# Gate/up of the last layer: the fourth product split into seven half-size ones, LayerNorm steps in three parts, w_down block sums behind the last row writes

## The chip, the cores and the metric

The kernel runs on one core of one Trainium2 chip. The metric is the device time of one execution in microseconds (us). The kernel before takes 1454.52 us, the median of three runs (1454.23 to 1454.56).

## What is computed

Two blocks alternate, A, B, A, B, over a residual stream x of 2048 tokens by 1024 channels (bf16). Every block sees the layer-normalised x and adds its result to x:

```
x = x + A(layernorm(x), wqkv, wo)      # linear attention, 32 heads
x = x + B(layernorm(x), w_gate, w_up, w_down)
x = x + A(layernorm(x), wqkv, wo)
x = x + B(layernorm(x), w_gate, w_up, w_down)

B: g = x @ w_gate; u = x @ w_up        # 1024 x 3584 each
   return (g * u) @ w_down             # 3584 x 1024
```

The same weights serve both B blocks. "First layer" and "last layer" below mean the first and second B block (with the A block ahead of each).

## The kernel before, in words

All work is recorded operation by operation in one list (class `_Prog`), each with the bytes and PSUM banks it reads and writes; waits are worked out from these. The order on every engine is the order of recording, so it is written out by hand, and every engine works strictly through its own list. All DMAs go through SyncE's list.

**The products of block B** use a Winograd form of Strassen's scheme: a 2x2 block product as seven block products. For a *pass* (`ps_` 0 or 1) of 1024 tokens, `gateup` handles 14 *pairs*; a pair is two column tiles of w_gate (even pairs) or of w_up (odd pairs). A pair has the products 1 to 7, each over half the inner dimension and 512 tokens: four matmuls of 128x512 for each of the two column tiles A and B (`pe`, L1070, matmuls at L1071). Partial sums live in PSUM: X (banks 0, 1), Y (2, 3), Z (4, 7). ScalarE copies them to SBUF scaled (`cp`, L1074 to L1076: P1, P6, P7 each write a buffer that `fin` adds later). `fin` (F1 to F4, L1078 to L1095, on VectorE at L691) writes a gate tile of h in even pairs, and in odd pairs multiplies the up tile into it, the product on GpSimd (L1095).

**Split products.** Some of the seven products are themselves done as seven half-size products (`l2_of`, L1152 on): each over a quarter of the inner dimension and 256 tokens, two matmuls of 128x256 (`mm`, L1174). Which ones is told by `L2SETS` (L200): in the last layer products 2, 5 and 4 of both passes, in the first layer none in pass 0 and 5, 4, 2 in pass 1. A split product has the steps 1, 5, 6, 7 and the two direct parts D..A (two half products) and D..B (one):

- step 1: half product into one of the shared banks 5 or 6 (`B_L2`), then ScalarE copies it as a seed to the target bank (L1178);
- step 5: half product into the other shared bank, then ScalarE copies it to SBUF (L1190);
- step 6: half product on top of that of step 1, then VectorE adds the SBUF copy to it into the target's second half (L1181);
- step 7: half product on top of that again, then a second seed copy (L1178) and a second addition (L1181);
- the direct half products go onto the seeded target banks.

The left operands of 3, 5, 6, 7 are block sums of the weights (`sums24` for products 2 and 4, `sums5` for product 5). The first layer makes them on VectorE and stores them in DRAM; the last layer loads them (`load_s24`, `load_s5`). The right operands 4, 5, 6 are token sums (`tp_ops`).

**The order around the change** is in the strings of `ORDERS` (L201 to L206), one for each set of split products. They are run once for each pair. `P6A` is product 6 of tile A with its copy, `21` step 1 of product 2, `D2A` its direct part for tile A, `F1A` the end of output 1, `S24` and `S5` the block sums, `R` two issues of weight loads, `T0` and `T1` the ticks for background work, `H` the hook (last pair alone); a quote mark means the token belongs to the pair before, a plus to the next one.

**Background work.** `ticks0` and `ticks1` (L1637, L1666) run LayerNorm steps: a step is two statistics of 512 channels (L447), an aggregate (L451), two tiny operations on GpSimd, and for an earlier row the normalising (L469, or L466 on ScalarE) and a transpose. They run a whole step in the ticks with `u % 4 < 2`, that is in both ticks of every even pair. In the first layer's pass 0 the ticks also make block sums of w_down (`wd_tick`), and the pair's own tokens make the seven-product sums of the weights of the next pair (`prep_s`).

**The down stage** (`down`) follows each pass: h times w_down, again seven products, four of them split (`DL2`, `l2prod`, matmuls at L1553), with the half products in the order `DOPS` = 1 5 6 2 7 3 4. Its operands are sums of blocks of h (`l2sums`), made on VectorE. The hook `pre` (L1461) makes the first four of them for product 1 at `H` in the last pair. The late tokens of the last pair (`tail`) are recorded behind the down stage's first half product.

Of the kernel before, what the change touches and what calls it, by code (L numbers as in the profile page):

```python
# [180 lines left out]
def build_kernel(nc, A_x, A_wqkv, A_wo, B_w_gate, B_w_up, B_w_down, out):  # L181
# [18 lines left out]
    L2SETS = {(False, 0): "", (False, 1): "542", (True, 0): "254", (True, 1): "254"}  # L200
    ORDERS = {  # L201
# [7 lines left out]
    DOPS = "1562734"  # L209
# [3 lines left out]
    PRE = "12"  # L213
# [69 lines left out]
    P = _Prog(V_SP + NJ * 64)  # L283
# [21 lines left out]
    KL5 = [dkey("l5%d" % i) for i in range(2)]  # L305
    KTA = [dkey("ta%d" % i) for i in range(2)]
# [11 lines left out]
    p5scr = nc.dram_tensor("p5_scratch", (NJ, 128, 1024), F16, kind="Internal").ap()  # L318
    nscr = nc.dram_tensor("xn_scratch", (S, D), F16, kind="Internal").ap()

    from contextlib import ExitStack
    with ExitStack() as es:
# [120 lines left out]
        def ln_a(i, mid=None):  # L443
            j = ln_cnt[0] % 8
            ln_cnt[0] += 1
            for h in range(2):
                P.add("dve", (lambda h: lambda e: e.bn_stats(st[j][:, 6 * h:6 * h + 6], x_res[:, i, (D // 2) * h:(D // 2) * (h + 1)]))(h),  # L447
                      rd=r_x(i, (D // 2) * h, (D // 2) * (h + 1)), wr=R(O_ST[j] + 24 * h, 24))
                if mid and h == 0:
                    mid()  # L450
            P.add("dve", lambda e: e.bn_aggr(mv[j][:, 0:2], st[j]), rd=R(O_ST[j], 48), wr=R(O_MV[j], 8))  # L451
# [21 lines left out]
        class LN:  # L473

            def __init__(self, to, order):
                self.to = to
                self.order = order
                self.q_b = []
                self.q_n = []
                self.q_t = []  # L480
                self.n = 0
                self.t_next = 0
                self.use_dma = False
                self.on_act = False
                self.depth = 2

# [8 lines left out]
            def start(self, i, mid=None):  # L495
                assert i == self.n
                j = ln_a(self.order[i], mid)
# [81 lines left out]
            def flush_step(self):  # L579
# [7 lines left out]
                if self.n < NST and self.pending_ab() < 3:  # L587
                    self.start(self.n)
# [133 lines left out]

        def tp_ops(pair, prods):
            s0 = pair * 1024
            res = []
            for q in prods:
                if q == "4":
                    x, base, st_ = T4, O_T + 8192, 1024
                elif q == "5":
                    x, base, st_ = T1, O_T, 1024  # L730
                else:
                    s1 = s0 + (512 if q == "3" else 0)
                    x, base, st_ = xblk(1, s1), O_XT + 4 * S * 2 + s1 * 2, S * 2
                o = O_TP[q]
                tp = [vh(o + i * 1024, 512).rearrange("p (k s) -> p k s", s=256) for i in range(3)]
                rt = [R(o + i * 1024, 1024) for i in range(3)]
# [25 lines left out]
        def load_s24(ps_, p):  # L762
            o = O_X + (8 * ps_ + 4) * D * 2 + p % 2 * 4096
            dma(vh(o, 2048), p4scr[p], R(o, 4096), KP4[p % 2], rd=R(V_SP + p * 64, 32))
# [7 lines left out]
        def load_s5(first, ps_, p):  # L772
            v, r = sp5buf(first, ps_, p % 2)
            dma(v, p5scr[p].rearrange("p (i x) -> p i x", i=4), [x for y in r for x in y], KL5[p % 2 if ps_ and not first else 0], rd=R(V_SP + p * 64 + 32, 32))
# [20 lines left out]
        def layer_A(lnp, nxt, first):  # L795
# [198 lines left out]
            for i in range(NST):  # L994
# [17 lines left out]
                if i in (11, 12, 13, 14):  # L1012
                    stash(i - 7)
                if i == 14 and not first:
# [5 lines left out]
                while RG["tn"] < 4 and nxt.t_next > 4 + RG["tn"]:  # L1020
                    RG["tq"] += t_ops(0, RG["tn"])
                    RG["tn"] += 1
                    if RG["tn"] == 4:
                        RG["tq"] += tp_ops(0, L2SETS[not first, 0])
# [7 lines left out]
        def layer_B(lnp, nxt, first):  # L1032
# [11 lines left out]
            def pair(ps_, p, l2):  # L1044
# [68 lines left out]
                ORDER = [q for q in "2543" if q in l2]  # L1113
                DST = {"5": Y, "2": Z, "4": Z if "4" in l2 else X, "3": Y}
# [657 lines left out]
```

## Time and profile before

| | |
|---|---|
| median of three runs | 1454.52 us (1454.23 to 1454.56) |
| the profiled execution | 1453.48 us, span from first to last instruction 1451.8 us |
| first layer: gate/up pass 0 | from 240.7 us, 170.7 us |
| first layer: gate/up pass 1 | from 494.5 us, 162.9 us |
| last layer: gate/up pass 0 | from 966.8 us, 159.7 us |
| last layer: gate/up pass 1 | from 1208.2 us, 158.8 us |
| TensorE matmuls | 8250: 2128 full-size ones of gate/up (L1071), 1764 half-size ones (L1174) |

How to read it: PE is TensorE, PEld its weight loads, DVE is VectorE, ACT ScalarE, POOL GpSimd, SP (or SPq) SyncE. A row of a timeline gives the start in us from the span's start, the length in us, engine, line of the kernel, operation, what is written and read, shape, how many alike follow each other, and in brackets the idle time of the engine ahead of it with what ended it. Matmuls overlap: the length of a row runs to the modelled end of its last matmul, so the pace of TensorE is read from the distance between starts.

### The profile page before, as it was taken

To read this page: it belongs to the slowest core of one execution; us is meant where nothing else is said; L and a number is where in the kernel's file an instruction comes from. 1 tells how busy PE (TensorE), PEld (TensorE's weight loads), DVE (VectorE), ACT (ScalarE), POOL (GpSimd) and SP (SyncE) were. 2 spreads that over 40 slices of the span, in tenths; PEclk is the share of its full clock that TensorE was granted. 3 is DMA by queue.
4 is the path that set the end of the run, shared out by engine and by line. 5 is a ranking of instruction groups with operands and counts; after the bars stand their busy time and mean duration, and the time that the engine had idled before them with its cause. 6 is when DMAs were issued, how large, how long until landed. Compare 5 with 4: busy or idle time off the path is not lost.

```text
span 1451.8 us, 22020 instructions
## 1 busy us (share of the span) xinstructions
PE 1442.6 (99%) x8250; PEld 793.5 (55%) x8250; DVE 1145.7 (79%) x2082; ACT 548.6 (38%) x1122; POOL 446.5 (31%) x435
## 2 busy tenths in 40 slices
PE   8999999999999999999999999999999999999999
PEld 4444444444444556665754444446666576666648
DVE  7986988888877797879789869896666986666787
ACT  3332355343400255551123323565555114555402
POOL 5553721222210043432035437214342201342400
DMA  6443757799999899775784646679777769888667
GB/s 232 101 107 103 155 117 187 246 315 312 311 331 305 296 278 288 251 260 194 248 250 111 180 103 156 160 185 269 257 250 250 248 235 287 280 276 271 208 220 234
DMA packets 344539, 329.14 MB, mean 227 GB/s; under 512 B 105200, under 2 KB 290800, under 8 KB 344432
## 3 DMA queue, kind: packets, MB, share of 16 engines
q1 hardware_dynamic: 344432, 327.73, 73.9%
q8 instruction: 65, 1.06, 0.3%
q14 instruction: 42, 0.34, 0.1%
HBM read 244.19 MB, written 62.65 MB: 211 GB/s over the span
## 4 chain that ended last, share of the span: by engine, by line
PE 96%; DVE 2%; DMA 2%; issue 0%; SPq 0%; POOL 0%; ACT 0%; DVEq 0%
PE ps L1071 30%; PE ps L804 15%; PE ps L1483 13%; PE ps L1174 13%; PE ps L1553 8%; PE ps L977 8%; PE ps L891 8%; DMA arena<-in_A_wqkv_dram 1%; DVE arena L447 1%; DMA arena<-in_A_x_dram 1%; PE ps L931 0%; PE ps L903 0%; DVE arena L691 0%; DMA arena<-in_B_w_up_dram 0%; DVE arena L688 0%
## 5 line engine op out<-in xcount | busy, mean ns | idle before, releaser
L1071 PE MATMUL ps<-arena 128*128 128x512 f16 x2128 | 508.1, 379 | 0.0
L691 DVE SCALAR_TENSOR_TENSOR arena<-ps,arena 128x512 f16<-128x512 f32 (+2 forms) x560 | 367.2, 684 | 90.9 <-PE ps L1483 30.5
L1095 POOL TENSOR_TENSOR arena<-arena 128x512 f16<-128x512 f16 x196 | 227.8, 1185 | 475.5 <-DVE arena L691 475.1
L1071 PEld LDWEIGHTS ps<-arena 128*128 128x128 f16 (+1 forms) x2128 | 206.9, 98 | 189.2 <-ACT arena L1076 4.4
L688 DVE TENSOR_TENSOR arena<-arena 128x512 f16<-128x512 bf16 (+6 forms) x532 | 296.4, 598 | 11.3 <-PE ps L1553 3.0
L1076 ACT ACTIVATE arena<-ps 128x512 f32<-128x512 f32 x308 | 184.3, 598 | 165.8 <-PE ps L1071 164.2
L1174 PE MATMUL ps<-arena 128*128 128x256 f16 x1764 | 242.7, 273 | 2.2 <-DVE ps L1181 1.9
L804 PE MATMUL ps<-arena 128*128 128x512 bf16 x1024 | 223.8, 379 | 2.2 <-ACT arena L549 0.9
L1174 PEld LDWEIGHTS ps<-arena 128*128 128x128 f16 (+1 forms) x1764 | 168.7, 98 | 92.0 <-DVE ps L1181 19.7
L1181 DVE TENSOR_TENSOR ps<-ps,arena 128x256 f32<-128x256 f32 x252 | 107.4, 429 | 111.6 <-ACT arena L1190 73.4
L1483 PE MATMUL ps<-arena 128*128 128x512 f16 (+1 forms) x896 | 194.2, 379 | 0.0
L804 PEld LDWEIGHTS ps<-arena 128*128 128x128 f16 x1024 | 99.5, 98 | 121.0 <-DMA arena<-in_A_wqkv_dram 1.5
L1178 ACT COPY ps<-ps 128x256 f32<-128x256 f32 x252 | 88.1, 363 | 175.7 <-PE ps L1174 122.3
L1483 PEld LDWEIGHTS ps<-arena 128*128 128x128 f16 x896 | 87.7, 98 | 105.1
L599 ACT ACTIVATE arena<-ps 128x512 f32<-128x512 f32 x128 | 76.5, 597 | 148.0 <-PE ps L804 125.4
L1553 PE MATMUL ps<-arena 128*128 128x256 f16 (+1 forms) x1176 | 129.9, 273 | 0.0
L1553 PEld LDWEIGHTS ps<-arena 128*128 128x128 f16 x1176 | 115.0, 98 | 14.6
L891 PE MATMUL ps<-arena 128*128 128x512 bf16 x512 | 115.4, 379 | 0.0
L977 PE MATMUL ps<-arena 128*128 128x512 bf16 x512 | 110.8, 379 | 0.0
L833 POOL TENSOR_TENSOR arena<-arena 128x1024 f16<-128x1024 f32 x32 | 79.8, 2494 | 90.3 <-DVE arena L831 83.6
L816 POOL TENSOR_TENSOR arena<-arena 128x512 f32<-128x512 f32 x60 | 76.4, 1274 | 80.2 <-DVE arena L602 78.0
L447 DVE BATCH_NORM_STATS2 arena<-arena 128x6 f32<-128x512 bf16 x128 | 88.2, 689 | 8.3 <-DMA arena<-in_A_x_dram 6.1
(56 smaller groups left out, 787.8 us busy)
## 6 DMA issues: line engine op xcount, KB each, us to landing
arena<-s_scratch SPq DMA_DIRECT2D x84, 512.0 KB, 5.7
arena<-d_images SPq DMA_DIRECT2D x36, 896.0 KB, 5.0
arena<-in_B_w_gate_dram SPq DMA_DIRECT2D x56, 512.0 KB, 4.9
arena<-in_B_w_up_dram SPq DMA_DIRECT2D x56, 512.0 KB, 5.4
arena<-t_scratch SPq DMA_DIRECT2D x20, 896.0 KB, 6.5
s_scratch<-arena SPq DMA_DIRECT2D x28, 512.0 KB, 5.7
arena<-p_scratch SPq DMA_DIRECT2D x28, 512.0 KB, 6.8
arena<-in_A_wqkv_dram SPq DMA_DIRECT2D x12, 1024.0 KB, 8.7
```

What stands on the lines that cost most here:

```text
L688: P.add("dve", lambda e: e.tensor_tensor(out=out, in0=a, in1=b, op=op), rd=rd, wr=wr, prd=prd)
L691: P.add("dve", lambda e: e.scalar_tensor_tensor(out=out, in0=a, scalar=sc, in1=b, op0=ALU.mult, op1=op1), rd=rd, wr=wr, prd=prd)
L804: return [e.matmul(psb(bank), xnT[:, k, i * 128:(i + 1) * 128], w[:, k, h * 512:(h + 1) * 512], start=(k == 0), stop=(k == KT - 1)) for k ...
L891: return [e.matmul(psb(bank), xr[:, t, j * 128:(j + 1) * 128], pk[:, h, t, :], start=(t == 0), stop=(t == NST - 1)) for t in range(NST)]
L977: return [e.matmul(psb(bank), xnT[:, g, i * 128:(i + 1) * 128], wp[:, g, dh * 512:(dh + 1) * 512], start=(dh == 0 and g == 0), stop=(g == ...
L1071: P.add("pe", lambda e: [e.matmul(psb(bank), w[:, k, :], x[:, k, :], start=(start and k == 0), stop=(k == 3), skip_group_check=True) for k ...
L1076: P.add("act", lambda e: e.activation(t, psb(bank), AF.Copy, scale=SG), prd=[bank], wr=r)
L1095: P.add(MUL_ENG, lambda e: e.tensor_tensor(out=hx, in0=ut, in1=hx, op=ALU.mult), rd=ur + hr, wr=hr)
L1174: P.add("pe", lambda e: [e.matmul(psb(bank)[:, 256 * half:256 * half + 256], w[:, k, :], xx[:, k, :], start=(start and k == 0), stop=(k == ...
L1181: P.add("dve", lambda e: e.tensor_tensor(out=psb(bank)[:, 256:512], in0=psb(src)[:, 0:256], in1=c5, op=ALU.add), prd=[src], rd=rc5, pwr=[b ...
L1483: return [e.matmul(psb(bank), hv[:, 7 * hf + k, t * 128:(t + 1) * 128], w[:, k, :], start=(q in fresh and hf == 0 and k == 0), stop=(hf == ...
L1553: P.add("pe", lambda e: [e.matmul(half(b, h), x[:, k, :], w[:, k, :], start=(bool(start) and k == 0), stop=(k == 6), skip_group_check=True ...
```

## The change

In words:

- `L2SETS`: both passes of the last layer split product 1 as well ("1254"), from the third pair on (in the first two pairs, whose block sums are not loaded, product 1 stays whole). Target banks are X. A new order string "1254" replaces "254".
- The first layer's pass 0 makes the block sums of product 1 too (token `S1` behind `S5`: four additions of 128x256 and a store of 256 KB for each pair), into DRAM `p1_scratch`. The last layer loads them (token `S1`, 12 loads a pass). The buffers are x rows 1 to 3 in pass 0 (stashed while the rows are written, loaded again at `HA` in the last pair) and the normalised tokens of pass 0 in pass 1.
- The token sums of product 1 (four additions) are made in the ticks of the first two pairs.
- LayerNorm: `micro` makes a step in three parts, one for each call: transpose and normalising; the first statistic; the second with the aggregate. The number of calls for each tick is written out in strings.
- The hook is two: `HA` makes the first two block sums of h, `HB` the other two, at different places of the last pair.
- The order "542" of the first layer's pass 1 is rearranged (`D2A` ahead of `51`, `S24` behind `41`, `S5` at the start).
- `DOPS` becomes 1 2 5 6 7 3 4; the addition that followed op 2 now follows op 6.

The core of the diff:

```
-    L2SETS = {(False, 0): "", (False, 1): "542", (True, 0): "254", (True, 1): "254"}
+    L2SETS = {(False, 0): "", (False, 1): "542", (True, 0): "1254", (True, 1): "1254"}
     ORDERS = {
-        "": "F3A' P1A D3B' P1B F3B' D2A F1A P6A D2B P6B P7A P7B R T0 P5A D4A D4B H F1B S5 F4A P5B F2A F4B F2B T1 D3A",
+        "": "F3A' P1A D3B' P1B F3B' D2A F1A P6A D2B P6B P7A P7B R T0 P5A D4A D4B HA HB F1B S5 S1 F4A P5B F2A F4B F2B T1 D3A",
...
-        "542": "F4A' 21 25 P1A D3B' F2A' T1' 26 P1B D4B' F3B' F4B' D3A' F3A' 27 51 D2A P6A F1A R D2B F1B 55 56 S24+ T0 P6B 41 H 57 P7A D5A 45 46 P7B D5B F2B 47 S5+ D4A",
-        "254": "D5B' 45' F2A' F2B' P1A 46' F1B' D3A' S24 F3A' S5 47' D4A' F4A' 21 D3B' P1B D4B' 25 26 F4B' T0 F3B' P6A 51 D2A F1A 27 R P6B 55 56 T1 H P7A 41 D2B 57 D5A P7B",
+        "542": "S5 21 F2A' 25 P1A T1' D3B' 26 P1B D4B' D3A' F3B' F4B' F3A' 27 D2A F1A R 51 P6A D2B 55 F1B 56 T0 P6B 41 S24+ HA 57 P7A D5A 45 46 P7B D5B HB F2B 47 D4A F4A",
+        "1254": "D5B' D3A' F2B' F3A' 47' 11 D4A' S1 15 16 D3B' F4A' 17 21 S5 D1A D4B' 25 F4B' D1B 26 F3B' T0 P6A 27 51 P6B 55 D2B F1B R HB' 56 P7A S24+ D2A F1A 57 41 D5A 45 F2A T1 P7B 46 HA",
     }
...
-    DOPS = "1562734"
+    DOPS = "1256734"
...
+            def micro(self, lim):
+                self.part += 1
+                if self.part % 3 == 1:
+                    self.step_t(1)
+                    self.b_one()
+                elif self.n < lim and self.half is None:
+                    if self.pending_ab() < 2:
+                        self.half = ln_cnt[0] % 8
+                        ln_cnt[0] += 1
+                        ln_stat(self.order[self.n], self.half, 0)
+                elif self.n < lim:
+                    self.start(self.n)
...
                 def prod(q, c):
                     if q == "1":
-                        pe("1", c, X[c], True)
+                        if "1" in l2 and p > 1:
+                            L["1"]["direct"](c)
+                        else:
+                            pe("1", c, X[c], True)
...
-                ORDER = [q for q in "2543" if q in l2]
-                DST = {"5": Y, "2": Z, "4": Z if "4" in l2 else X, "3": Y}
+                ORDER = [q for q in "12543" if q in l2]
+                DST = {"1": X, "5": Y, "2": Z, "4": Z if "4" in l2 else X, "3": Y}
...
-                def pre():
+                def pre(which):
                     if "1" in l2:
-                        for k in PRE:
-                            for i in range(2):
-                                need(("s", "1", int(k) - 1, i))
+                        for i in range(2):
+                            need(("s", "1", "AB".index(which), i))
...
             def ticks0(u):
-                if u % 4 < 2 and not lnp.done():
-                    lnp.flush_step()
+                for _ in range(int(("3300330033003300330033003300" if first else "0000011111011122111111112110")[u])):
+                    if not lnp.done():
+                        lnp.micro(NST)
...
-                if u % 4 < 2 and not is_last and nxt.t_next < LN_G1:
-                    nxt.step_t(1)
-                    nxt.b2_one()
-                    nxt.b1_one()
-                    if nxt.n < LN_G1 and nxt.pending_ab() < 3:
-                        nxt.start(nxt.n)
+                if not is_last:
+                    for _ in range(int("1111111012010211121101111111"[u])):
+                        if nxt.t_next < LN_G1:
+                            nxt.micro(LN_G1)
```

More of the change, by code (lines that the diff above doesn't have):

```diff
@@ L485, in __init__ @@
                 self.depth = 2
+                self.half = None
+                self.part = 0
             def dst(self, n):
@@ L1013, in layer_A @@
                     stash(i - 7)
+                    if not first and i > 11:
+                        stash(i - 11)
                 if i == 14 and not first:
@@ L1248, in token @@
                         p, tk = p + 1, tk[:-1]
-                    if tk == "H":
+                    if tk[0] == "H":
                         if p == NP - 1:
-                            hook()
+                            hook(tk[1])
+                            if "1" in l2 and not ps_ and tk == "HA":
+                                for i in range(1, 4):
+                                    dma(x_res[:, i, :], xscr[i * 128:(i + 1) * 128, :], r_x(i), KX[i], rd=R(V_X + i * 32, 32))
                         return
@@ L1270, in token @@
                     c = pairs[p]
+                    if tk == "S1" and not first and p < 2:
+                        return
                     if not first and (tk == "S24" and p < 2 or tk == "S5" and p < 1 + ps_) or first and ps_ and tk[0] == "S" and p == 0:
```

100 lines of the change are left out of this document (68 added, 32 removed).

## Prediction

> **What bounds the kernel now.** I read the page's busy times, its chain that ended last, the windows of the stages that the change touches, and the waits of TensorE.
>
> ```profile
> PE 1442.6 (99%) x8250; PEld 793.5 (55%) x8250; DVE 1145.7 (79%) x2082; ACT 548.6 (38%) x1122; POOL 446.5 (31%) x435
> PE 96%; DVE 2%; DMA 2%; issue 0%; SPq 0%; POOL 0%; ACT 0%; DVEq 0%
> ```
> ```profile
> 240.70:411.40 170.70, 170.70 (x792) 76.22 (x791) 141.51 (x314) 66.88 (x114) 34.24 (x31) 1.00 0.91 289
> 494.50:657.40 162.90, 161.39 (x1034) 98.76 (x1033) 134.74 (x267) 88.63 (x210) 60.36 (x59) 1.00 0.84 266
> 966.80:1126.50 159.70, 159.13 (x1022) 99.14 (x1020) 104.85 (x207) 88.78 (x210) 57.62 (x53) 1.00 0.77 242
> 1208.20:1367.00 158.80, 158.69 (x1023) 99.30 (x1020) 99.45 (x194) 87.04 (x208) 55.79 (x49) 1.00 0.81 269
> ```
> ```profile
> PE ps L1174 <- DVE ps L1181: 1.9, 4, 0.7
> ```
>
> TensorE carries 96% of the chain and hardly ever waits: the longest sum of its waits is 1.9 us. So only two things move the time: the columns that TensorE streams, and new (or vanished) waits of TensorE. The four windows (start and end, length, then busy time and instructions of TensorE's matmuls, its weight loads, VectorE, ScalarE and GpSimd, granted clock, DMA share, GB/s) are the gate/up passes, in order: first layer, pass 0 and 1; last layer, pass 0 and 1. The clock is full (1.00) in all, and the last layer has room on VectorE (105 of 160 us) and ScalarE (89); the first pass has little (142 of 171, DMA share 0.91).
>
> A pair of the last layer, in steady state, and the delays that a chain is made of:
>
> ```profile
> 1283.81 1.26 PE L1174 MATMUL ps<-arena 128*128 128x256 f16 x10
> 1284.51 0.65 ACT L1178 COPY ps<-ps 128x256 f32<-128x256 f32 x2
> 1285.19 0.43 DVE L1181 TENSOR_TENSOR ps<-ps,arena 128x256 f32<-128x256 f32 x1 [1.08 <-ACT ps L1178]
> 1285.77 0.60 PE L1174 MATMUL ps<-arena 128*128 128x256 f16 x4
> 1286.20 1.03 PE L1071 MATMUL ps<-arena 128*128 128x512 f16 x4
> 1287.07 0.38 PE L1174 MATMUL ps<-arena 128*128 128x256 f16 x2
> 1291.40 1.03 PE L1071 MATMUL ps<-arena 128*128 128x512 f16 x4
> 1291.44 0.37 ACT L1190 COPY arena<-ps 128x256 f32<-128x256 f32 x1
> 1291.91 0.43 DVE L1181 TENSOR_TENSOR ps<-ps,arena 128x256 f32<-128x256 f32 x1 [1.88 <-ACT arena L1190]
> 1292.27 1.04 PE L1174 MATMUL ps<-arena 128*128 128x256 f16 x8
> 1292.47 0.60 ACT L1076 ACTIVATE arena<-ps 128x512 f32<-128x512 f32 x1 [0.66 <-PE ps L1071]
> 1292.96 0.74 ACT L1178 COPY ps<-ps 128x256 f32<-128x256 f32 x2
> 1295.31 0.93 PE L1174 MATMUL ps<-arena 128*128 128x256 f16 x7
> ```
>
> From starts, not durations: four half-size matmuls take 0.43 us (1285.77 to 1286.20), four full ones 0.87 (to 1287.07). A pair is 32 full and 42 half ones and takes 11.50 us (1283.81 to 1295.31); one half is so 0.109 and one full 0.216. The result of a matmul can be read about 0.16 after its slot (1.03 against 0.87), and ScalarE starts 0.04 later (1291.40 + 1.03 = 1292.43 to 1292.47): 0.20 from the slot's end. A full-bank copy holds ScalarE 0.49 (1292.47 to 1292.96), a half one runs 0.35 to 0.38. VectorE's seed addition starts 0.10 after the copy to SBUF (1291.81 to 1291.91), 0.03 after a seed copy (1285.16 to 1285.19), and runs 0.43.
>
> **The change, part by part.**
>
> *Columns.* From the third pair of each last-layer pass on, product 1 is 14 half matmuls in place of 8 full ones: 8 x 0.216 - 14 x 0.109 = 0.20 us less, in 2 x 12 pairs: **-4.8 us**. The Trainium skill ("TensorE: Matmul & The Clock Gate", Back-to-back issue gap) gives for streams of weight load and matmul 81 ns at 128 and 131 ns at 512 columns, so halving would not halve; a line between them (an estimate) gives 98 ns at 256, and 14 x 98 - 8 x 131 = 0.3 us more a pair. This trace disagrees with it on this point: 109 against 216.
>
> *New waits in these pairs.* The added work fits: per pair three half copies (1.1 us) and two seed additions (0.9) in 11.3 us. But product 1 now has the chain of a split product (step 1: copy to the seed; step 5: copy to SBUF; 6: seed addition; 7: second seed and addition; then the direct matmuls), and four products take turns in the two banks 5 and 6. I counted TensorE's work between the ends of each chain in the new order. DVE to TensorE costs 0.05:
>
> ```profile
> 973.92 1.41 DVE L447 BATCH_NORM_STATS2 arena<-arena 128x6 f32<-128x512 bf16 x2
> 975.50 0.41 DVE L1181 TENSOR_TENSOR ps<-ps,arena 128x256 f32<-128x256 f32 x1
> 975.96 0.61 PE L1174 MATMUL ps<-arena 128*128 128x256 f16 x4 [0.47 <-DVE ps L1181]
> ```
>
> - 15 to 17: needed 0.20 + 0.37 + 0.10 + 0.43 + 0.05 = 1.15; between them stand 16 (0.22) and D3B' (0.86) = 1.08. Short by 0.07, a little more as 16 itself waits some 0.02 for the seed copy of 11, which queues behind that of 47'.
> - 17 to D1B: needed 0.20 + 0.36 + 0.03 + 0.43 + 0.05 = 1.07; between: 21, D1A, D4B', 25, ten halves = 1.09. Just enough.
> - P6A to D2B: the seed of 27 queues on ScalarE behind the copy of P6A: 0.20 + 0.49 + 0.38 + 0.03 + 0.43 + 0.05 = 1.58; between: 27, 51, P6B, 55 = 1.52. Short by 0.07 with unrounded slots.
>
> The same sum for the old order (25 to D2A: 26, P6A, 51 = 1.30 against 1.22 with a queue of 0.06) leaves 0.08; the rows give D2A at 1292.49 (third of the eight from 1292.27) and the addition's end at 1292.34, less 0.05: 0.10. So the method holds to some 0.02 a chain. Together 0.15 a pair (bounds 0.08 and 0.25): 24 x 0.15 = 3.6, and the third chain alone in the four direct pairs, 0.3: **+3.9** (2.2 to 6.4). Behind a waiting TensorE everything waits, so each counts in full; ScalarE and VectorE have 2 us or more to spare a pair and catch up. So most of the gain in columns is eaten by chains that are short by a tenth.
>
> *LayerNorm in three parts, and the hook in two.* The rows at 973.92 show a step's two statistics (1.4 us) ahead of a seed addition, and TensorE waiting for that. So it is in the first layer's second pass, where the last two rows below are the hook's four w_down sums and what waits for them:
>
> ```profile
> 525.25 0.54 DVE L469 TENSOR_SCALAR arena<-arena 128x1024 f16<-128x1024 bf16 x1
> 525.71 1.42 DVE L447 BATCH_NORM_STATS2 arena<-arena 128x6 f32<-128x512 bf16 x2
> 527.75 0.94 PE L1174 MATMUL ps<-arena 128*128 128x256 f16 x6 [0.75 <-DVE ps L1181]
> 503.69 1.05 PE L1174 MATMUL ps<-arena 128*128 128x256 f16 x7 [0.30 <-DVE ps L1181]
> 653.07 2.23 DVE L688 TENSOR_TENSOR arena<-arena 128x896 f16<-128x896 f16 x4 [0.88 <-POOL arena L1095]
> 655.70 1.05 PE L1174 MATMUL ps<-arena 128*128 128x256 f16 x7 [0.39 <-DVE ps L1181]
> ```
>
> The bracket leaves out the result's 0.16, so these three cost 0.91, 0.46 and 0.55; smaller ones beside them I put at 0.5. A third of a step is at most half of what stood there (0.7 to 0.8 us), two sums are 1.1 in place of 2.2: that is more than each wait. Of 2.4 us I take **-2.0** (-1.2 to -2.4), since the block sums of product 2 still share that stretch. In the last layer the wait at 975.96 (0.63) goes, and waits of 0.1 to 0.3 at the starts and ends of both passes may: -1.3. Against it stands a load: at the start of the last pass TensorE waits for the block sums of product 5:
>
> ```profile
> 1208.17 1.03 PE L1071 MATMUL ps<-arena 128*128 128x512 f16 x4
> ...
> 1212.43 1.03 PE L1071 MATMUL ps<-arena 128*128 128x512 f16 x4
> 1213.57 0.60 PE L1174 MATMUL ps<-arena 128*128 128x256 f16 x4
> ```
>
> that is 1213.57 - 1212.43 - 0.86 = 0.28. The load's place in SyncE's queue stays, but step 55 comes sooner in the new order: 4.54 us after the pass's start (four full groups, five half pairs) in place of 5.13 (1213.30 less 1208.17, the first slot of the pass), as D2A stands behind it and not ahead: +0.6. Together **-0.7** (-1.3 to 0).
>
> *Block sums of product 1 in the first pass.* Per pair four more 128x256 additions on VectorE and a store of 256 KB. The like block of product 5 is the second row:
>
> ```profile
> 298.47 0.68 DVE L691 SCALAR_TENSOR_TENSOR arena<-ps,arena 128x512 f16<-128x512 f32 x1
> 299.64 0.69 DVE L691 SCALAR_TENSOR_TENSOR arena<-ps,arena 128x512 f16<-128x512 f32 x1 [0.48 <-PE ps L1071]
> 334.17 2.48 DVE L691 SCALAR_TENSOR_TENSOR arena<-ps,arena 128x512 f16<-128x512 f32 x4 [0.48 <-PE ps L1071]
> 356.44 1.01 DVE L688 TENSOR_TENSOR arena<-arena 128x256 f16<-128x256 f16 x4
> 358.35 1.89 DVE L691 SCALAR_TENSOR_TENSOR arena<-ps,arena 128x512 f16<-128x512 f32 x3 [0.89 <-PE ps L1071]
> 382.52 0.69 DVE L691 SCALAR_TENSOR_TENSOR arena<-ps,arena 128x512 f16<-128x512 f32 x1 [0.48 <-PE ps L1071]
> ```
>
> The fourth is: some 0.95 us. It stands ahead of F4A, F2A in the up pairs and of F2A in the gate pairs, and D3A waits for F2A. In an up pair F4A starts 0.20 after the slot of D4A, F2A ends 1.28 later, and D3A stands 1.73 behind D4A: 0.2 to spare. Idle time ahead of F4A absorbs the rest: 0.89 (358.35) is enough, 0.48 (334.17, 382.52) leaves 0.3 each. In the gate pair at 298.47 F2A already runs late: it ends at 299.15 and D3A starts at 299.44 (0.20 before F2B), so 0.95 - 0.24 = 0.7. Two alike and one of these: **+1.4** with 0.1 for pairs that are just enough; lower bound 0, and upper bound 5 where the stores (7% more traffic on a share of 0.91) make weight loads land later: VectorE's preparation for the next pair waits for these.
>
> *At nothing.* In the split w_down products op 2 now follows op 1, and 7 follows 6: the copy between needs 0.20 + 0.37 + 0.05, the other row block's seven halves cover 0.76. If that is gone it is 0.1 in 24 places. The loads of product 1's sums (256 KB, 24 of them) queue on SyncE ahead of product 5's sums and of the next weights; they wait for D1A of the pair before and have 8 us to land. Reloads of three x rows at the end of pass 0 have over 8 us before their eviction.
>
> **Sum.** -4.8 + 3.9 - 2.0 - 0.7 + 1.4 = **-2.2 us**. The profiled execution took 1453.48 us (span 1451.8), 1.04 less than the median of 1454.52; so 1451.3 against the first and **1452.3** against the median.
>
> **Rivals.**
> 1. *The chains are not short* (0.03 a pair: ScalarE or VectorE hands over sooner than my sums): 3.9 becomes about 0.8, the sum -5.3, **1449.2**. For it: the margins are of the size of my error; against: the old order's margins come out right.
> 2. *VectorE becomes the bound of the first pass.* Place: D3A waiting for F2A; price: 0.95 - 0.2 = 0.75 in each of the seven up pairs, where the idle 0.5 to 0.9 ahead of F4A is used up, about 5.3, plus 0.7; it decides from the point where weight loads land about 0.8 us later than now. The sum becomes -2.2 - 1.4 + 6.0 = +2.4, and with 0.35 in the gate pairs +5: **1457 to 1459**, slower. For it: 142 + 13 of 171 us and the share 0.91; against: the windows of the trace show no TensorE wait there now.
> 3. *The chains are short by 0.3*: +3.6 more, +1.4: **1455.9**, no measurable change.
> 4. *Half matmuls cost more than half.* The page's mean durations are 379 and 273 ns:
>
> ```profile
> L1071 PE MATMUL ps<-arena 128*128 128x512 f16 x2128 | 508.1, 379 | 0.0
> L1174 PE MATMUL ps<-arena 128*128 128x256 f16 x1764 | 242.7, 273 | 2.2 <-DVE ps L1181 1.9
> ```
>
> If these were the price, 24 x (14 x 0.273 - 8 x 0.379) = +19 us, **1471**. The start distances speak against it. The Trainium skill's section named above points the same way, with a smaller loss.
>
> **Chances.** A measurement of this kernel tells about 0.2% (2.9 us) from no change. Forecast 0.53 (own range 1450.5 to 1454), rival 1 0.28, rival 2 0.13, rival 3 0.05, rival 4 0.01. Faster by over 0.2% (below 1451.6): most of rival 1 and a sixth of the forecast's range, 0.34; slower (above 1457.4): most of rival 2, and 4: 0.13; within 0.2%: 0.53. Range 1448.8 to 1457.
>
> **What would show it.** On TensorE 8394 matmuls in place of 8250 (24 x 8 full ones less, 24 x 14 halves more); pairs of the last layer 11.44 us apart in place of 11.50, with 0.07 at 17 and at D2B; no wait by LayerNorm in 494 to 657; waits of 0.3 to 0.7 at three D3A in 240 to 411; a wait of 0.9 at the start of the last pass. The forecast is wrong if the first pass is over 3 us longer, or if the pair distance is 11.3 or above 11.55.

## The result, and the profile after

The changed kernel takes **1458.15 us** (median of nine runs, 1457.51 to 1459.35), the kernel before 1454.23 on the same chip (nine runs, 1452.87 to 1456.52): ratio 1.0029, 95% interval 1.0019 to 1.0039. It is 3.9 us slower; 2.2 us faster was forecast, and 1457.0 was the upper end of the range.

The page of the changed kernel, its busy times and its chain that ended last:

```profile
PE 1442.2 (99%) x8337; PEld 796.9 (55%) x8394; DVE 1184.5 (81%) x2194; ACT 572.0 (39%) x1194; POOL 446.3 (31%) x435
...
PE 92%; DMA 4%; DVE 2%; SPq 1%; issue 1%; ACT 0%; DVEq 0%; ACTq 0%
```

8394 weight loads are the 8394 matmuls forecast (57 matmul records are missing). The busy time of TensorE has not grown, and its share of the chain fell from 96% to 92%: the loss is waiting, and half of what took its place is DMA. The waits of TensorE by what it waited for (us in total, times, longest) name the load:

```profile
PE ps L1231 <- DMA arena<-p_scratch: 2.8, 4, 1.4
```

`p_scratch` is the block sums that the first layer stores. The windows of the four gate/up passes (columns as for the kernel before) tell where:

```profile
242.40:412.10 169.70, 168.81 (x781) 74.80 (x780) 152.26 (x369) 66.84 (x114) 31.78 (x29) 1.00 0.95 307
497.60:657.30 159.70, 159.70 (x1028) 98.66 (x1027) 132.56 (x264) 88.28 (x210) 59.51 (x58) 1.00 0.85 270
968.00:1126.60 158.60, 158.60 (x1092) 100.29 (x1091) 118.32 (x233) 100.29 (x247) 59.13 (x56) 1.00 0.82 267
1209.70:1371.60 161.90, 159.06 (x1092) 100.42 (x1091) 113.51 (x219) 98.73 (x244) 57.19 (x51) 1.00 0.85 280
```

The last pass has the largest hole: 159.06 of 161.90 us busy. The first pass has a smaller one (168.81 of 169.70), the waits for the new block sums that were forecast there. Cut from TensorE's first matmul of a stage to its first of the next, the two traces and those of three experiments below compare like this (us):

| stage | before | after | s1_ahead | sums_ahead | sums_ahead_gate |
|---|---|---|---|---|---|
| ahead of the first gate/up | 240.73 | 242.37 | 241.50 | 241.23 | 240.76 |
| first layer: gate/up 0 | 168.35 | 169.76 | 169.77 | 169.79 | 169.20 |
| first layer: down 0 | 85.47 | 85.47 | 85.47 | 85.47 | 85.47 |
| first layer: gate/up 1 | 162.14 | 159.67 | 159.77 | 159.68 | 159.65 |
| down 1 and the second A block | 310.15 | 310.68 | 310.77 | 310.75 | 310.73 |
| last layer: gate/up 0 | 158.81 | 158.62 | 162.26 | 158.04 | 157.18 |
| last layer: down 0 | 82.53 | 83.17 | 83.17 | 83.18 | 83.62 |
| last layer: gate/up 1 | 158.04 | 161.91 | 158.04 | 158.04 | 156.82 |
| last layer: down 1 | 85.55 | 85.66 | 85.68 | 85.67 | 86.13 |

From the first gate/up on, after less before is +1.41 - 2.47 + 0.53 - 0.19 + 0.64 + 3.87 + 0.11 = +3.9 us, what the medians show. The 1.6 us ahead of it belong to this one execution, since the kernels of the other three columns have the same code there and reach that stage at 240.76 to 241.50. The window of its first 15 us has a granted clock of 0.77, where that of before has 1.00; in the profiled executions of the kernels below it is 0.89 or 1.00.

```profile
0.00:15.00 15.00, 10.84 (x41) 4.63 (x42) 6.95 (x14) 3.97 (x5) 4.86 (x22) 0.77 0.91 291
```

Now the hole itself. TensorE's timeline of the changed kernel around the worst of the four waits:

```profile
1242.67 1.04 PE L1231 MATMUL ps<-arena 128*128 128x256 f16 x8
1245.06 0.61 PE L1231 MATMUL ps<-arena 128*128 128x256 f16 x4 [1.36 <-DMA arena<-p_scratch]
```

Eight half products from 1242.67 end their slots at 1243.54, and the next (steps 15 and 16, the first users of product 1's sums) start at 1245.06: 1.52 us late. SyncE's timeline of the same kernel shows when that load was issued, and behind what:

```profile
1234.74 0.38 SPq L422 DMA_DIRECT2D arena<-in_B_w_gate_dram  x1
1235.17 0.58 SPq L422 DMA_DIRECT2D arena<-s_scratch  x1
1235.79 0.43 SPq L422 DMA_DIRECT2D arena<-p_scratch  x1
1236.27 0.43 SPq L422 DMA_DIRECT2D out_dram<-arena  x1
1236.74 1.71 SPq L422 DMA_DIRECT2D arena<-p_scratch  x2
```

The first of the last two is the load of product 1's sums. Two weight loads of 512 KB each (the second half of `R`, which waited for a slot of the ring of weight buffers), the sums of products 2 and 4, and a finished output row stand ahead of it. Issued at 1236.74 and needed at 1243.54, it had 6.8 us and took 8.3. Its own buffer had been free since 1207. The same happens at 1268.86 (0.79 us), 1304.13 (0.75) and 1339.08 (0.43), where the buffer had been free for 12 us when the second half of `R` went out: 3.5 us together.

### The profile page after: what moved, and what is told of

It is laid out like the page before. It is cut to its first block, busy times and chain, and to the rows that moved or that the text cites. A ratio compares the mean times of both kernels' runs of the same rounds, so it can differ in the third digit from the quotient of the medians.

```text
span 1457.3 us, 22537 instructions
## 1 busy us (share of the span) xinstructions
PE 1442.2 (99%) x8337; PEld 796.9 (55%) x8394; DVE 1184.5 (81%) x2194; ACT 572.0 (39%) x1194; POOL 446.3 (31%) x435
## 4 chain that ended last, share of the span: by engine, by line
PE 92%; DMA 4%; DVE 2%; SPq 1%; issue 1%; ACT 0%; DVEq 0%; ACTq 0%
PE ps L1113 25%; PE ps L844 15%; PE ps L1231 15%; PE ps L1548 13%; PE ps L1618 8%; PE ps L1017 8%; PE ps L931 8%; DMA arena<-p_scratch 2%; DVE arena L712 1%; DMA arena<-in_A_wqkv_dram 1%; SPq L422 1%; DVE arena L715 1%; DMA arena<-in_B_w_gate_dram 1%; PE ps L943 0%; PE ps L971 0%
## 5 line engine op out<-in xcount | busy, mean ns | idle before, releaser
L1113 PE MATMUL ps<-arena 128*128 128x512 f16 x1936 | 463.6, 379 | 1.3 <-DVE arena L715 1.1
L715 DVE SCALAR_TENSOR_TENSOR arena<-ps,arena 128x512 f16<-128x512 f32 (+2 forms) x560 | 372.2, 684 | 101.7 <-PE ps L1231 41.4
L712 DVE TENSOR_TENSOR arena<-arena 128x512 f16<-128x512 bf16 (+6 forms) x596 | 311.7, 565 | 18.0 <-PE ps L1618 10.1
L1231 PE MATMUL ps<-arena 128*128 128x256 f16 x2100 | 279.9, 273 | 2.8 <-DMA arena<-p_scratch 2.8
L1238 DVE TENSOR_TENSOR ps<-ps,arena 128x256 f32<-128x256 f32 x300 | 128.4, 430 | 64.1 <-ACT ps L1235 24.8
L1235 ACT COPY ps<-ps 128x256 f32<-128x256 f32 x300 | 100.9, 361 | 186.1 <-PE ps L1231 158.4
```

Of the source, the lines that this page charges most:

```text
L712: P.add("dve", lambda e: e.tensor_tensor(out=out, in0=a, in1=b, op=op), rd=rd, wr=wr, prd=prd)
L715: P.add("dve", lambda e: e.scalar_tensor_tensor(out=out, in0=a, scalar=sc, in1=b, op0=ALU.mult, op1=op1), rd=rd, wr=wr, prd=prd)
L1113: P.add("pe", lambda e: [e.matmul(psb(bank), w[:, k, :], x[:, k, :], start=(start and k == 0), stop=(k == 3), skip_group_check=True) for k ...
L1231: P.add("pe", lambda e: [e.matmul(psb(bank)[:, 256 * half:256 * half + 256], w[:, k, :], xx[:, k, :], start=(start and k == 0), stop=(k == ...
L1238: P.add("dve", lambda e: e.tensor_tensor(out=psb(bank)[:, 256:512], in0=psb(src)[:, 0:256], in1=c5, op=ALU.add), prd=[src], rd=rc5, pwr=[b ...
```

## The experiments

All compare with the kernel before on the same chip. The theory from these traces: the last layer loses to the *place* of that load in SyncE's list. The rival: to the *traffic*, 3 MB more for each pass over DMA engines that are busy for a share of 0.82 and 0.85 with it.

### s1_ahead: product 1's load ahead of the weights

```
-... 47' 11 D4A' S1 15 16 ... D2B F1B R HB' 56 ...
+... 47' 11 D4A' 15 16 ...    D2B F1B S1+ R HB' 56 ...
```

> The changed kernel (1458.15 us), in which the load of product 1's block sums is issued earlier in the last layer: by the pair before, ahead of its two issues of weight loads (R), and no more behind them. Theory (place): in the last pass the load stands in SyncE's list behind the second of these weight loads, which waits for a ring slot that comes free 13 to 20 us after the sums' own buffer; from there it needs some 8 us and lands 0.4 to 1.5 us too late in four pairs. The four waits (3.5 us together) go and nothing takes their place: 1454.6 us, 0.9976 of the changed kernel, level with the kernel before. The 0.05 at step 15, 0.08 at step 17 and 0.08 at D2B remain in each pair. Rival (traffic): the DMA share is 0.97 to 0.99 in the first half of that pass, and 3 MB of sums are new; if the queues are the limit, another load (product 2 and 4's sums, or weights) lands late in place of this one, and 2 to 3.5 us of waits stay: 1456.5 to 1458.

Measured: **1457.35 us**, ratio 1.0017 (1.0008 to 1.0025). That is in the rival's range, and the load that is late now is the one that the rival named, the sums of products 2 and 4. But it is late in the other pass, which neither had. (The share of 0.97 to 0.99 that the rival starts from is 0.89 in the trace, from 1210 to 1290 us.) The windows of the last layer's two passes:

```profile
967.30:1129.50 162.20, 158.85 (x1091) 100.69 (x1090) 118.21 (x232) 100.77 (x246) 58.98 (x55) 1.00 0.85 262
1212.70:1370.70 158.00, 158.00 (x1092) 100.18 (x1090) 113.52 (x219) 98.73 (x244) 57.15 (x51) 1.00 0.88 287
```

In the last pass the theory holds: all four waits are gone and nothing takes their place, at a DMA share of 0.88, higher than before. It is 158.04 us long, 3.87 less where 3.5 was forecast, as the 0.05 at step 15 goes too. In pass 0 the opposite: 3.6 us more, now at step 25, the first user of the sums of products 2 and 4. TensorE's row, then SyncE's:

```profile
1004.49 0.71 PE L1231 MATMUL ps<-arena 128*128 128x256 f16 x5 [0.79 <-DMA arena<-p_scratch]
```
```profile
992.04 0.32 SPq L422 DMA_DIRECT2D arena<-p_scratch  x1
992.40 0.45 SPq L422 DMA_DIRECT2D arena<-in_B_w_up_dram  x1
992.89 0.58 SPq L422 DMA_DIRECT2D arena<-s_scratch  x1
993.51 0.44 SPq L422 DMA_DIRECT2D arena<-in_B_w_gate_dram  x1
994.00 1.77 SPq L422 DMA_DIRECT2D arena<-s_scratch  x1
995.81 8.02 SPq L422 DMA_DIRECT2D arena<-p_scratch  x3
```

and SyncE's of the changed kernel at the same place, with the pair's own four weight loads:

```profile
990.22 0.38 SPq L422 DMA_DIRECT2D arena<-in_B_w_up_dram  x1
...
992.97 0.38 SPq L422 DMA_DIRECT2D arena<-in_B_w_gate_dram  x1
...
994.02 0.91 SPq L422 DMA_DIRECT2D arena<-p_scratch  x2
```

In pass 0 product 1's sums have one buffer, so the load waits for D1A of the pair that issues it, until 992.04. In SyncE's list everything behind it waits too: the weights that went out from 990.22 on now go in one block from 992.40, and the next sums stand behind 2 MB and land at 1004.4, where 994.02 plus 6 was early enough. This points to the order, with a second way to get it wrong, but the traffic is not yet ruled out: the bytes are the same, and 3.6 us of waits came back.

### sums_ahead: both loads of sums ahead of the weights

```
-... D2B F1B R HB' 56 P7A S24+ D2A ...
+... D2B F1B S1+ S24+ R HB' 56 P7A D2A ...
```

> The changed kernel with the loads of product 1's sums and of those of products 2 and 4 both issued by the pair before, ahead of its weight loads (R), in both passes of the last layer; the same bytes as before. The weights have 10 to 18 us to spare there, the sums 0 to 4. Theory (a queue lands its loads in the order of issue, and what is needed soonest stands behind what is needed last): no wait for a load of sums in either pass, 158.5 us from the start of gate/up to that of the down stage in pass 0 (162.3 with only product 1's load ahead) and 158.0 in pass 1: 1454.3 us, 3.9 less than the changed kernel's 1458.15, level with the kernel before (ratio 1.000). Rival (traffic: 3 MB more a pass at a share of 0.82 to 0.87 are themselves the limit): now the weights or product 5's sums land late, 2 to 4 us of waits stay: 1456.5 to 1458.

Measured: **1453.91 us**, ratio 0.9997 (0.9988 to 1.0006), as the theory had it; against the changed kernel 4.2 us less with the same bytes. The windows of the two passes:

```profile
966.90:1125.00 158.10, 158.10 (x1092) 100.32 (x1091) 118.38 (x233) 100.28 (x247) 59.07 (x56) 1.00 0.87 269
1208.20:1366.20 158.00, 158.00 (x1093) 100.20 (x1091) 113.50 (x219) 98.76 (x245) 57.24 (x51) 1.00 0.92 287
```

TensorE is without a hole in both, at a DMA share of 0.87 and 0.92. The traffic rival is out. The weights that these pairs load land 3.8 us or more ahead of their use even now, so being last costs them nothing. The Trainium skill ("DMA: Bandwidth & Descriptors", Queues, rings and completion order) says that each DMA engine consumes a ring's descriptors in order; it does not promise that they complete in order. In this trace the 182 loads of the two passes, all issued by SyncE, land in the order of their issue without an exception, so the most urgent load has to be issued first.

### first_layer_only and sums_only: the first layer's two parts

The first is the changed kernel with `"254"` in the last layer, no sums of product 1 made or loaded, the old `DOPS`, and whole LayerNorm steps in `ticks0` as before; so steps in three parts are left in the first layer's pass 1 alone. The second is the kernel before plus `S1` behind `S5` in the order of the first pass.

> Of the change only the LayerNorm steps in three parts (first layer and the pass in which the next block's steps begin), the hook in two parts and the new order of the first layer's pass 1; product 1 whole everywhere, no sums of product 1, the last layer and the down stage as before. Theory: the first layer's pass 1 gets 2.5 us shorter (2.47 between the traces) and nothing else moves: 1451.8 us, 0.9983 of the kernel before. Rival: 0.4 to 0.5 us of it come back as waits in the tail of that pass and in the down stage behind it: 1452.2 to 1452.4; a second rival, that the 2.5 us belong to the new order of half products in the down stage: then 1454.2, no change.

> The kernel before, in which the first layer's pass 0 also makes the block sums of product 1 and stores them (14 times four additions and 256 KB); nobody loads them, so this is added work only. Theory: 1.4 us at three D3A (0.9, 0.2, 0.2), which wait for F2A: 1455.6 us, 1.0010 of the kernel before. Rival (the stores crowd the weight loads, and VectorE becomes the bound of the pass): 5 us or more, 1459; second rival: the waits come from elsewhere in the change, no difference, 1454.2.

Measured: **1452.02 us** (ratio 0.9981, 0.9973 to 0.9990) and **1455.72 us** (1.0008, 0.9999 to 1.0017). The first lies between the theory (1451.8) and its first rival (1452.2 to 1452.4), the second on the theory's number, though its interval does not rule out no change. So the traces decide. The window of the first layer's pass 1 in the first, and of pass 0 in the second:

```profile
495.40:655.10 159.70, 159.70 (x1028) 98.64 (x1027) 131.94 (x264) 88.25 (x210) 59.51 (x58) 1.00 0.86 270
```
```profile
241.10:410.80 169.70, 168.80 (x781) 74.82 (x780) 152.24 (x369) 66.84 (x114) 31.78 (x29) 1.00 0.96 307
```

In the first, pass 1 has no hole left (159.70 of 159.70) and is 2.47 us shorter, as forecast. The first rival is right as well: 0.10 at D3B and 0.43 at D3A of the last pair come back, and the down stage behind takes 81.56 us in place of 81.00. That the total is still near the theory is luck: the last layer's two gate/up passes are 0.28 and 0.27 shorter in this execution, with the code of before. The second rival is out, since `DOPS` is the old one here. In the second, 1.42 us are lost in pass 0, at the same three D3A as in the changed kernel. Its pass 1 was also 2 us longer in the profiled execution than before (164.12), in waits for seed additions behind LayerNorm steps, which that kernel still has whole; the median, 1.2 us above before, does not show that.

### old_down_order: DOPS undone

```
-    DOPS = "1256734"
+    DOPS = "1562734"
```

> The changed kernel with the old order of the half products of w_down (1 5 6 2 7 3 4, the addition behind op 2). Theory: the new order costs some 0.6 us in the last layer's first down pass (waits of 0.1 and 0.4 for ScalarE's copies and 0.45 at its start) and nothing in the other three: 1457.5 us, 0.9996 of the changed kernel, hardly to be measured; the trace shows that down pass 82.5 us long as before and not 83.2. Rival: the waits stay with the old order too, as they come from the late rows of gate/up: 1458.1. Second rival: the new order covers a copy that the old one waited for in the other down passes: 1459.

Measured: **1461.23 us**, ratio 1.0043 (1.0030 to 1.0055): 3.1 us above the changed kernel, so my theory fell. The second rival has the direction, but not the cause: what the old order waits for are sums of h, not copies. The hook's second half (`HB`) now runs in the tail of the last pair, and with the old order op 6 comes too early for its sums. TensorE's timeline at the start of the down stage:

```profile
1130.75 2.24 PE L1618 MATMUL ps<-arena 128*128 128x256 bf16 x19
1133.35 0.92 PE L1618 MATMUL ps<-arena 128*128 128x256 f16 x7 [0.36 <-issue]
1134.88 1.36 PE L1618 MATMUL ps<-arena 128*128 128x256 f16 x11 [0.61 <-DVE arena L712]
```

That is 0.5 and 0.8 us in both down stages of the last layer, where the new order leaves one wait of 0.45 at op 7 (and in pass 0 the 0.5 at product 3): the two down stages are 0.3 and 0.85 us longer. The last layer's gate/up passes are 1.1 and 1.4 longer, with waits for loads of sums: of product 1's, five of 0.2 to 0.4 in pass 0 in place of one of 0.1, and six in place of four in pass 1, with 0.7 for product 5's at its start. Nothing in the edit moves these loads. In the changed kernel those of pass 0 land 0.05 to 1.1 us ahead of use, so a little decides; why they come later in this kernel is not settled.

### sums_ahead_56: step 56 ahead of D2B, and product 1's sums behind F2A

```
-... 55 D2B F1B S1+ S24+ R HB' 56 P7A ...      (last layer)
+... 55 56 D2B F1B S1+ S24+ R HB' P7A ...
-... F1B S5 S1 F4A P5B F2A F4B F2B ...         (first pass)
+... F1B S5 F4A P5B F2A S1 F4B F2B ...
```

> The kernel of sums_ahead with two more moves: step 56 ahead of D2B (D2B then has 0.22 more of TensorE's work ahead of it, where it waits 0.08 in each pair), and in the first layer's pass 0 the sums of product 1 behind F2A, and not ahead of F4A. Theory: the pairs of the last layer come 11.44 us apart in place of 11.515 (24 split pairs and the four whole ones, 0.077 each: 2.1 us), and the waits of D3A in the first pass go (1.4, to 168.4 us): 1454.3 - 3.5 = 1450.8, ratio to the kernel before 0.9975; this would be faster than both kernels. Rival 1 (the pair is not bound by that chain: the 0.08 comes back at step 57 or P7A): 1452.9. Rival 2 (the first pass is bound by VectorE's sum of work, so the wait moves from D3A to D3B): 1452.2. Both: 1454.3.

Measured: **1459.83 us**, ratio 1.0039 (1.0027 to 1.0052). The two edits part in the trace. The last layer's passes fell to 156.83 and 157.35 us. But the first pass grew to 176.11: the wait moved to D3B, as rival 2 has it, but with 7.8 us where 1.4 were, which rival 2 did not have. VectorE's rows at one of the up pairs, then the second of the four additions by itself with GpSimd's product beside it, then TensorE's:

```profile
262.68 0.68 DVE L715 SCALAR_TENSOR_TENSOR arena<-ps,arena 128x512 f16<-128x512 f32 x1
263.27 1.99 DVE L712 TENSOR_TENSOR arena<-arena 128x256 f16<-128x256 bf16 x4
265.18 1.28 DVE L715 SCALAR_TENSOR_TENSOR arena<-ps,arena 128x512 f16<-128x512 f32 x2
```
```profile
263.47 1.27 DVE L712 TENSOR_TENSOR arena<-arena 128x256 f16<-128x256 bf16 x1
```
```profile
263.43 1.15 POOL L1137 TENSOR_TENSOR arena<-arena 128x512 f16<-128x512 f16 x1 [6.58 <-DVE arena L715]
```
```profile
266.52 1.68 PE L1113 MATMUL ps<-arena 128*128 128x512 f16 x7 [1.04 <-DVE arena L715]
```

The four additions (1.99 us here, where I had counted 0.95) stand between F2A and F4B, F2B; F2B ends at 266.46, and D3B waits for it, 1.2 us in each of six up pairs. But the other three of the four take 0.28 each, as all four do ahead of F4A. The second takes 1.27, 0.98 more, while a product runs on GpSimd from 263.43 to 264.58. That is so in all seven up pairs. In the gate pairs, which have no product on GpSimd, no addition is slow, and only one of them waits (0.5 at D3A of the fifth pair). So most of the new wait is not VectorE's sum of work, but an addition that comes beside GpSimd's product; ahead of F4A, where VectorE would have been idle, it does not.

### sums_ahead_gate: the same, with the sums moved in the gate pairs alone

```
+... F1B S5 SU F4A P5B F2A SG F4B ...      SU: up pairs; SG: gate pairs; neither in pairs 0, 1
```

> The kernel of sums_ahead with step 56 ahead of D2B, and in the first layer's pass 0 the sums of product 1 behind F2A in the gate pairs alone (in the up pairs ahead of F4A, as in the changed kernel); the sums of the first two pairs, which nobody loads, are left out. Theory: the last layer's passes get 1.2 and 0.7 to 1.2 us shorter, as in sums_ahead_56 (the pairs 11.44 us apart), and in the first pass the 1.05 us at the fourth gate pair goes, while the two waits of 0.18 in up pairs stay: 1453.9 - 2.2 - 1.0 = 1450.7, ratio to the kernel before 0.9973, faster than both kernels. Rival (VectorE is the bound of the gate pairs too, as it was of the up pairs): D3B waits there instead, by up to 1.2 us in each of six pairs, 1452 to 1459.

Measured: **1452.53 us**, ratio 0.9986 (0.9977 to 0.9995): faster than both kernels, by less than forecast (0.9973). The last layer's passes are 0.86 and 1.22 us shorter than in sums_ahead; 1.2 and 0.7 to 1.2 were forecast. But the two down stages behind them are 0.45 longer each, since D3B of the last pair now waits 0.69 in place of 0.24, a term that the sum did not have. The first pass is 169.20 us, 0.59 less where 1.0 was forecast: the wait in the fifth pair (the gate pair that is meant) fell from 1.05 to 0.11, while one in an up pair grew from 0.18 to 0.54. The pair distance shows the chain waits as they are. First the changed kernel, TensorE's rows of a pair of the last pass without a late load:

```profile
1317.04 1.92 PE L1231 MATMUL ps<-arena 128*128 128x256 f16 x16
...
1320.95 0.91 PE L1231 MATMUL ps<-arena 128*128 128x256 f16 x6
1321.70 0.59 PE L1113 MATMUL ps<-arena 128*128 128x512 f16 x2
...
1326.25 1.52 PE L1231 MATMUL ps<-arena 128*128 128x256 f16 x12
1327.61 1.03 PE L1113 MATMUL ps<-arena 128*128 128x512 f16 x4
1328.55 0.72 PE L1231 MATMUL ps<-arena 128*128 128x256 f16 x5
```

17 starts at 1317.04 and again at 1328.55: 11.51 us apart. At 0.109 for a half and 0.216 for a full matmul, six halves from 1320.95 end at 1321.61 and the next starts at 1321.70 (D2B waited 0.08); twelve from 1326.25 end at 1327.56, next 1327.61 (step 15 waited 0.05); four full ones from there end at 1328.47, next 1328.55 (step 17 waited 0.08). Then sums_ahead_gate:

```profile
1298.45 1.92 PE L1231 MATMUL ps<-arena 128*128 128x256 f16 x16
...
1302.37 0.82 PE L1231 MATMUL ps<-arena 128*128 128x256 f16 x6
1303.02 1.03 PE L1113 MATMUL ps<-arena 128*128 128x512 f16 x4
...
1307.58 1.50 PE L1231 MATMUL ps<-arena 128*128 128x256 f16 x12
1308.91 1.03 PE L1113 MATMUL ps<-arena 128*128 128x512 f16 x4
1309.83 1.92 PE L1231 MATMUL ps<-arena 128*128 128x256 f16 x16
```

11.38 apart: D2B waits no more (1302.37 + 0.655 = 1303.02), step 15 neither (1307.58 + 1.31 = 1308.89, with 0.01 at step 16), step 17 still 0.06 (1308.91 + 0.863 = 1309.77).

### hook_in_tail: HA behind F4A of the last pair

```
-... D3B' F4A' 17 21 ... T1 P7B 46 HA
+... D3B' F4A' HA' 17 21 ... T1 P7B 46
```

> The kernel of sums_ahead_gate with the first half of the hook (the two block sums of h of HA) behind F4A of the last pair, and not ahead of its F2B. Theory: in both passes of the last layer D3B of the last pair waits 0.69 for F2B, since VectorE first makes HA's two sums (1.46 and 0.61); both waits go, the wait of 0.45 at op 7 of the down stage stays: 1452.5 - 1.4 = 1451.1, ratio to the kernel before 0.9977. Rival: VectorE has no time to spare between the two stages, and the sums made later hold up op 5 or op 6 of the down stage instead by as much: 1452.5.

Measured: **1456.95 us**, ratio 1.0019 (1.0009 to 1.0028). The rival's cause, at another place and dearer. The profiled execution is the shortest of the eleven (1454.51); it is 3.2 us longer than that of sums_ahead_gate, 0.97 and 0.96 of it in the two down stages, where the edit acts. What else the median has, 1456.95, no trace shows. TensorE's rows:

```profile
1127.79 1.47 PE L1622 MATMUL ps<-arena 128*128 128x256 bf16 x12
1131.29 1.92 PE L1622 MATMUL ps<-arena 128*128 128x256 bf16 x16 [2.02 <-ACT ps L1628]
```

The waits at D3B are gone, and that at op 7 too, but F4B now stands behind HA's sums, the bank that it empties is the target of op 1's seed copy, and op 2 waits 2.2 us for that copy, in both passes. So between these two stages VectorE is the bound, and of the two orders tried the one that frees the PSUM bank first is the better.

## Why the prediction was wrong, step by step

Forecast were -2.2 us, measured +3.9. Of the 6.1 between them 3.5 are the loads of product 1's sums, about 1.5 the chain waits and 0.8 the starts and ends of the last layer; the two errors in the first layer cancel. With the loads in time the kernel is level with the one before (sums_ahead, 0.9997), not faster, so the later terms mattered too.

- **Columns**, -4.8: right. A pair's slots give 56 x 0.1092 + 24 x 0.2159 = 11.30 us against 11.49 before; 0.20 a pair.
- **Chain waits**, +3.9 (0.15 a pair): mis-sized. 17 and D2B were named and wait 0.08 each, 0.07 forecast. The third, 0.05 at step 15, I had put down as 0.02 at step 16. Together 0.21 a pair where 0.15 was forecast, so the split pair gained nothing: 11.517 us apart in place of 11.492, where 11.44 was forecast. In sums_ahead, with the load issued by the pair before, step 15's wait is gone, 16 waits 0.02, 17 0.06 and D2B 0.08 (11.475): 0.16, so there the sums of latencies came out to 0.01. What they lacked is the 0.05 at step 15. It is not a late landing: the last pair's load landed 1.58 us before its use, and step 15 waited 0.05 there too; why, no run settles.
- **LayerNorm in three parts, hook in two**, -2.0 in the first layer: right in size, -2.47. At the pass's end 0.10 and 0.43 of it come back (D3B and D3A of the last pair, behind the hook), the +0.53 of the stage behind. No run parts the steps in thirds from the hook in two and the new order of that pass.
- **Starts and ends of the last layer**, -0.7: wrong, about 0. The wait at 975.96 is gone with smaller ones, 1.9 us of waits in all, but 2.0 came in their place: the hook's sums cost 0.24 at D3B of each last pair and 0.45 at op 7, with 0.5 at op 2 of product 3 in pass 0. The two down stages got 0.64 and 0.11 longer, although two half products fewer (45, 46: 0.44) stand in the tail. The load wait forecast at the start of the last pass (0.9) did not show in this execution; it did in two others (0.7 and 0.5 at step 55).
- **Block sums in the first pass**, +1.4: right, +1.41 by trace and +1.2 by median (sums_only), though shared out otherwise (1.0, 0.2, 0.2 for 0.7, 0.3, 0.3).
- **"At nothing", the loads of product 1's sums**: this is the step that failed, +3.5 us. I gave them "8 us to land" from D1A of the pair before. But an issue on SyncE is not bound to its own buffer alone. In the last pass, where the sums have two buffers and D1A of the pair before did not matter, it stood behind `R`, whose second load waits for a ring slot. That left 6.8 us. And 8 was not ample either: the worst load took 8.3, and in the last pass of the kernel before the medians from issue to landing were already these:

```profile
arena<-p_scratch SPq DMA_DIRECT2D x13, 512.0 KB, 6.8
...
arena<-p_scratch SPq DMA_DIRECT2D x13, 256.0 KB, 7.0
```

- **"At nothing", the order of the half products**: right for this kernel only because the order belongs to the hook in two parts; without it the down stages lose another 0.3 and 0.8 us (old_down_order).
- **Rivals.** None was this one. Rival 2 gave 1457 to 1459, and the time that came out lies in it by coincidence: it was for VectorE in the first pass, which lost 1.4 as the forecast has it. A loss of that size can be had there (7.8 us in sums_ahead_56, 6.0 in the rival), but mostly from additions beside GpSimd's product; ahead of F4A there is none.

With the loads in order and one step moved (sums_ahead_gate) the last layer's passes gain 1.6 and 1.2 us on the kernel before, its down stages give back 1.1 and 0.6, and the first pass 0.85. First_layer_only, without product 1 split at all, is as fast (0.9981 against 0.9986, intervals overlap). So in the orders tried here the fourth split product is worth nothing measurable, and the part of the change that gains is the first layer's pass 1: LayerNorm in thirds, the hook in two and the new order, which no run takes apart.

## What to carry to other kernels

Before a new load is costed at nothing, write down three times from the trace: when it is really issued (the latest wait of anything ahead of it in the issuing engine's list), how long loads of its size take to land in that very stretch, and when the first user comes; then issue loads in the order of their spare time, the least first. An issue that has to wait for its buffer holds up every issue behind it, so it must not stand ahead of anything urgent. And a split that saves 0.2 us a pair must be checked against chains counted to 0.02, since three chains short by 0.05 to 0.08 ate all of it. Last, before work is moved on VectorE, see from the trace what GpSimd does at the new place.

## What the runs showed of the hardware

- In these traces a VectorE addition of two SBUF operands is held up by a GpSimd product beside it. An addition of 128x896 takes 0.62 us alone (median of 87 in the trace of the kernel before) and 0.88 to 1.57 where it meets products (the other 9); the product then takes up to 1.53 in place of 1.15. In sums_ahead_gate there are two alike at the end of a pass, the first beside products on GpSimd that ran until 1124.50. VectorE's two rows, then GpSimd's:

```profile
1123.53 1.46 DVE L712 TENSOR_TENSOR arena<-arena 128x896 f16<-128x896 f16 x1
```
```profile
1124.91 0.61 DVE L712 TENSOR_TENSOR arena<-arena 128x896 f16<-128x896 f16 x1
```
```profile
1121.12 3.38 POOL L1137 TENSOR_TENSOR arena<-arena 128x512 f16<-128x512 f16 x3 [13.23 <-DVE arena L715]
```

The Trainium skill ("SBUF — State Buffer", Who interferes with whom) says that a VectorE instruction with two SBUF inputs contends with a GpSimd instruction that reads SBUF; this agrees, and so does the addition at 263.47 in sums_ahead_56 (1.27 in place of 0.28). The 0.69 at D3B in sums_ahead_gate stands behind the first of these rows.
- A half matmul (256 columns) costs 0.1092 us and a full one (512) 0.2159 between starts, in all ten traces at a granted clock of 1.00: a half is 1.2% dearer than half.
